# A dual-stream attention block on one core: where the text V gets its shift, where the text gate's rows are computed, and the order of three weight loads

## The chip, the core and the metric

The kernel runs on one core of a Trainium2 chip. The metric is the device time of one execution in microseconds (us). Five runs of the kernel before gave 118.70 to 119.60 us, median 119.28 us. One more execution was recorded by the hardware profiler; it took 118.92 us, of which the trace spans 116.8 us.

The engines are called as in the profile: PE is TensorE (matmuls), PEld its loading of weights, DVE is VectorE, ACT is ScalarE, POOL is GpSimd and SP is SyncE, which issues most of the DMAs. PSUM is the memory that matmuls write to, SBUF the one that everything else works in.

## What is computed

Two streams of tokens, image (2 x 256 tokens) and text (2 x 32 tokens), of width D = 1152, attend to each other. For each stream a conditioning vector c gives a shift, a scale and a gate; the normalised tokens are scaled and shifted, projected to Q, K and V, attended jointly, projected again, gated, and added to the input.

```python
mod_i = (_silu(c) @ wmod_img).reshape(B, 6, 1, D)
mod_t = (_silu(c) @ wmod_txt).reshape(B, 6, 1, D)
shi, sci, gai = (mod_i[:, 0].copy(), mod_i[:, 1].copy(), mod_i[:, 2].copy())
sht, sct, gat = (mod_t[:, 0].copy(), mod_t[:, 1].copy(), mod_t[:, 2].copy())
hi = _layernorm(x_img, axis=-1) * (1 + sci) + shi
ht = _layernorm(x_txt, axis=-1) * (1 + sct) + sht
qkvi = hi @ wqkv_img
qkvt = ht @ wqkv_txt
...
scores = jnp.einsum('bqd,bkd->bqk', q, k) * D ** (-0.5)
p = _softmax(scores, axis=-1)
a = jnp.einsum('bqk,bkd->bqd', p, v)
at, ai = (a[:, :Nt].copy(), a[:, Nt:].copy())
out_i = x_img + gai * (ai @ wo_img)
out_t = x_txt + gat * (at @ wo_txt)
```

All matrices are bfloat16. The weights that are read come to some 37 MB of the 39.4 MB that the core reads in all.

## The kernel before, in words

**Weights.** Fourteen blocks of 1152 x 1152 are read once each, into five slots of SBUF that are used again and again (`wtile(slot)`). All are issued on SP's queue, in the order of lines 103 to 122; an issue whose slot is still being read waits, and all later ones wait behind it. `load_w` (L89) issues a block whole or in column pieces, `load_rows` (L97) in three pieces of three row groups. The last five are `w_ga_i` (image gate, slot 0), `w_v_t` (text V, slot 1), `w_ga_t` (text gate, slot 2), `w_o_i` (image output, slot 3) and `w_o_t` (text output, slot 1 again).

**Order of work.** All matmuls go through `mm` (L61) and all transposes through `tr` (L64), which keep TensorE in program order. The other engines are put in order by the framework; where `pin` is written the program's order holds there too. The stages of TensorE are: image V (to 34 us), image Q and K in 18 groups of nine matmuls of 512 columns (`qk_img`), with text work hung between the groups (the `hooks`), text Q and K (`qk_txt`), scores, text V, attention, output.

**The text shift.** The row of the text shift is not made on TensorE: `vec_part` multiplies and adds the weights on VectorE, 18 operations on 128 x 1152 into `acc_sh` (L417, L419), in three parts that are hooks. `vec_split` cuts the sum into two bfloat16 halves (L426 on ACT, L427 on VectorE), which 16 small matmuls (`vec_rows`) bring into a row form. The text layernorm (`txt_ln`) and its transposes are two more hooks.

**The shift of V.** Image V is computed from the scaled input without the shift; its contribution `svc`, the shift times the V weights, is added to the attention's result when that leaves PSUM (L610, L612): each row of probabilities sums to one, so the shift passes through. Text V is computed from the shifted input, and so must have the image's `svc` taken away first. `shift_v_rows` keeps that row as `svr`, in PSUM's layout of four groups of columns. In `v_txt` the product of `hT_t` and `w_v_t` is followed by two matmuls per half with `sel`, a matrix of 0 and -1, that subtract `svr` inside PSUM (L489); four copies, alternating between VectorE (L184) and ACT (L186), bring the result to `v_t`, and L494 copies it to partitions 64 to 127.

**Tiled matmuls.** Where only 64 or 32 columns of TensorE are needed, two or four matmuls are given different column tiles (`tile_position`): text V and the text output two of 64 columns, the gates' rows and the shift rows four of 32 columns.

**The gates.** `mod_rows` (L496) makes a gate's row from `sT32` (the silu of c, padded to 32 columns) with 36 matmuls, copies it to SBUF and writes it to a DRAM scratch `gsc` (L505) from POOL's queue; DMAs on the same queue then spread it: `gb` for the image (L514), `gbf` for the text (L523). `xf` is the text input in the layout of the text output (L519).

**After the scores.** Softmax (`softmax_tile`, L542 to L551) leaves probabilities in four image tiles and `pbt` for the text. `p_transposes(b)` transposes nine blocks for one image b and copies them to `pT`, on VectorE for image 0 (L595), on ACT for image 1 (L597). Attention runs in three groups: six key matmuls on `v_i`, then six on `v_t`, then six more on `v_i`. The output follows: `out_img` for four tiles of 128 tokens, each three groups of nine matmuls of 384 columns, which VectorE multiplies with the gate (L650) and adds to the input (L651). The text output `out_txt` stands between the third and the fourth.

Of the kernel before, what the change touches and what calls it, by code (L numbers as in the profile page):

```python
# [14 lines left out]
def kernel(  # L15
# [14 lines left out]
    nc = tc.nc  # L30
    bf = mybir.dt.bfloat16
    f32 = mybir.dt.float32
    PSUM = bass.MemoryType.PSUM

    B, NI, D = x_img.shape
    NT = x_txt.shape[1]
    P = 128
    KT = D // P
# [3 lines left out]
    NTT = B * NT  # L42
    CH = 384
    NCH = D // CH
    VC = 288
# [5 lines left out]
    act = ctx.enter_context(tc.tile_pool(name="act", bufs=1))  # L51
    const = ctx.enter_context(tc.tile_pool(name="const", bufs=1))
    work = ctx.enter_context(tc.tile_pool(name="work", bufs=2))
    small = ctx.enter_context(tc.tile_pool(name="small", bufs=4))
    ps_mm = ctx.enter_context(tc.tile_pool(name="ps_mm", bufs=6, space=PSUM))
    ps_tr = ctx.enter_context(tc.tile_pool(name="ps_tr", bufs=2, space=PSUM))
# [3 lines left out]
    def mm(*a, **k):  # L60
        return pin(nc.tensor.matmul(*a, **k))  # L61
# [22 lines left out]
    def load_w(slot, src, c0, splits=(D,)):  # L84
        t = wtile(slot)
        sv = wview(src, c0)
        o = 0
        for n in splits:
            nc.sync.dma_start(t[:, :, o:o + n], sv[:, :, o:o + n])  # L89
            o += n  # L90
        return t

    def load_rows(slot, src, c0):
        t = wtile(slot)
        sv = wview(src, c0)
        for r0 in range(0, KT, 3):
            nc.sync.dma_start(t[:, r0:r0 + 3, :], sv[:, r0:r0 + 3, :])  # L97
        return t
# [13 lines left out]
    w_q_i = load_w(3, wqkv_img, 0)  # L112
    w_sh_t = load_rows(0, wmod_txt, 0)
    w_k_i = load_w(4, wqkv_img, D)
# [2 lines left out]
    w_k_t = load_w(3, wqkv_txt, D)  # L117
    w_ga_i = load_w(0, wmod_img, 2 * D)
    w_v_t = load_w(1, wqkv_txt, 2 * D)
    w_ga_t = load_w(2, wmod_txt, 2 * D)  # L120
    w_o_i = load_rows(3, wo_img, 0)
    w_o_t = load_rows(1, wo_txt, 0)

    nc.scalar.preload_act_table_set("natural_log_exp_and_others")
# [4 lines left out]
    NGG = 4  # L129
    LW = P // NGG  # L130
# [11 lines left out]
    sT32 = const.tile([P, KT, 32], bf)  # L142
# [39 lines left out]
    def evac(out_ap, in_ap):  # L182
        if evac_idx[0] % 2 == 0:
            nc.vector.tensor_copy(out_ap, in_ap)  # L184
        else:
            nc.scalar.copy(out_ap, in_ap)  # L186
        evac_idx[0] += 1
# [39 lines left out]
    def mod_cols_of(gps, name):  # L227
        t = const.tile([P, KT, LW], f32, name=name, tag={"shtc": "scc", "sctc": "shc"}.get(name, name))
        pin(nc.vector.transpose(t[:].rearrange("p c l -> p (c l)"), gps[:].rearrange("p c l -> p (c l)")))
        return t  # L230
# [141 lines left out]
    def qk_img(wq, blk, hooks):  # L372
        for j in range(KT):
            for hook in hooks.get(j, ()):
                hook()
            ps = ps_mm.tile([P, B * NI], f32, tag="mm")
            for kt in range(KT):
                mm(ps[:], lhsT=wq[:, kt, j * P:(j + 1) * P], rhs=hT_i[:, kt, :],
                   start=(kt == 0), stop=(kt == KT - 1))
            qk_evac(qkT[:, blk * KT + j, :, 0:NI], ps[:].rearrange("p (b n) -> p b n", b=B), blk)  # L380

    gsc = tc.dram_tile([2, B, D], bf, name="mod_scratch")
    sel = const.tile([P, NGG, NTT], bf)
    nc.gpsimd.tensor_scalar(sel[:].rearrange("p g (b t) -> p g b t", b=B),
                            ident[:].rearrange("p (g r) -> p g r", g=NGG)[:, :, 0:B].unsqueeze(3)
                            .to_broadcast([P, NGG, B, NT]), -1.0, None, op0=ALU.mult)
    v_t = act.tile([P, D], bf)
    svr = act.tile([P, KT, LW], bf)
    rows, cols = {}, {}

    def shift_v_rows():
        p_sv = mod_rows_of(w_v_i, shT32)
        nc.scalar.copy(svr[:], p_sv[:])
        cols["v"] = mod_cols_of(p_sv, "svc")

    xT_t = act.tile([P, KT, NTT], bf)
# [44 lines left out]
    def txt_shift_part(r0, r1):  # L441
        return lambda: vec_part(nc.vector, w_sh_t, acc_sh, r0, r1, range(B))
# [38 lines left out]
    def v_txt():  # L481
        for r in range(2):
            ps = ps_mm.tile([P, KT, LW], f32, tag="mm")
            for kt in range(KT):
                for g in range(2):
                    mm(ps[64 * g:64 * g + NTT], lhsT=hT_t[:, kt, :], rhs=group(w_v_t, kt, 2 * r + g),
                       start=(kt == 0), stop=False, tile_position=(0, 64 * g))
            for g in range(2):
                mm(ps[64 * g:64 * g + NTT], lhsT=sel[:, 2 * r + g, :], rhs=svr[:],  # L489
                   start=False, stop=True, tile_position=(0, 64 * g))  # L490
            for g in range(2):
                evac(v_t[0:NTT, :].rearrange("p (c g l) -> p g c l", g=NGG, l=LW)[:, 2 * r + g],
                     ps[64 * g:64 * g + NTT])
        nc.vector.tensor_copy(v_t[64:64 + NTT, :], v_t[0:NTT, :])  # L494

    def mod_rows(w_blk, si):  # L496
        gps = ps_mm.tile([P, VC], f32, tag="mm")
        for kt in range(KT):
            for g in range(NGG):
                mm(gps[32 * g:32 * g + 32, :], lhsT=sT32[:, kt, :], rhs=w_blk[:, kt, g * VC:(g + 1) * VC],  # L500
                   start=(kt == 0), stop=(kt == KT - 1), tile_position=(0, 32 * g))
        g_sb = work.tile([P, VC], bf, tag="garow")
        evac(g_sb[:], gps[:])
        for b in range(B):
            nc.gpsimd.dma_start(gsc[si, b, :].rearrange("(g j) -> g j", g=NGG), g_sb[b:P:32, :])  # L505

    gb = act.tile([P, B, D], bf, tag="Bt")
    gbf = act.tile([P, 2, VC], bf)
    xf = act.tile([P, 2, VC], bf)

    def img_gate():
        mod_rows(w_ga_i, 0)
        for b in range(B):
            nc.gpsimd.dma_start(gb[:, b, :], gsc[0, b, :].partition_broadcast(P))  # L514

    def txt_gate():
        mod_rows(w_ga_t, 1)
        for g in range(2):
            pin(nc.gpsimd.dma_start(xf[64 * g:64 * g + NTT, :, :],  # L519
                                    xt_flat.rearrange("t (r g j) -> g t r j", r=2, g=2)[g]))  # L520
            for b in range(B):
                r0 = 64 * g + 32 * b
                nc.gpsimd.dma_start(gbf[r0:r0 + NT, :, :],  # L523
                                    gsc[1, b, :].rearrange("(r g j) -> g r j", r=2, g=2)[g].partition_broadcast(NT))

    v_last()
    shift_v_rows()
    qk_img(w_q_i, 0, {1: (txt_ln,), 2: (txt_shift_part(0, 3),), 5: (txt_shift_part(3, 6),),
                      6: (txt_transposes,), 8: (txt_shift_part(6, KT),)})
    qk_img(w_k_i, 1, {1: (txt_shift_split,),  # L530
                      6: (txt_rows_scale, txt_rows_shift, txt_cols_shift, txt_modulate),
                      8: (lambda: qk_txt(0, w_q_t),)})
    qk_txt(1, w_k_t)
# [21 lines left out]
    def scores_img(b):  # L555
        for qi in range(TPB):
            q0 = qi * P
            sps = ps_mm.tile([P, NTOK], f32, tag="mm")
            for ft in range(KT):
                mm(sps[:], lhsT=qkT[:, ft, b, q0:q0 + P], rhs=qkT[:, KT + ft, b, :],  # L560
                   start=(ft == 0), stop=(ft == KT - 1))
            softmax_tile(sps, P, (b, qi), [(0, P, b)])
# [15 lines left out]
    def p_transposes(b):  # L578
        pT_ps = ps_tr.tile([P, 8 * P], bf, tag="tr")

        def one(kj, pb, qp, perm):
            o = kj * NTOK + qp
            tr(pT_ps[:, o:o + P], pb[:, kj * P:(kj + 1) * P], perm[:])

        for kj in range(3):
            if b:
                one(kj, pbs["t"], qpos[b][2], ident2)
            for qi in range(TPB):
                one(kj, pbs[(b, qi)], qpos[b][qi], ident)
            if not b:  # L590
                one(kj, pbs["t"], qpos[b][2], ident)
        pT_v = pT_ps[:, 0:3 * NTOK].rearrange("p (k n) -> p k n", k=3)
        pT = work.tile([P, 3, NTOK], bf, tag="pT")
        if b == 0:
            nc.vector.tensor_copy(pT[:], pT_v)  # L595
        else:
            nc.scalar.copy(pT[:], pT_v)  # L597
        pTs[b] = pT
# [29 lines left out]
    scores_img(0)  # L628
    scores_txt()
    img_gate()  # L630
    scores_img(1)
    v_txt()
    p_transposes(0)
    p_transposes(1)
    txt_gate()
    for d0 in range(0, KT, 3):
        attn_pair(*[[(b, dt) for dt in range(d0, d0 + 3)] for b in range(B)])

# [17 lines left out]

    def out_txt():
        of = work.tile([P, 2, VC], bf, tag="of", bufs=1)
        for r in range(2):
            ps = ps_mm.tile([P, VC], f32, tag="mm")  # L660
            for dt in range(KT):
                for g in range(2):
                    c0 = (2 * r + g) * VC
                    mm(ps[64 * g:64 * g + NTT, :], lhsT=aT[:, dt, NI:NI + NTT], rhs=w_o_t[:, dt, c0:c0 + VC],
                       start=(dt == 0), stop=(dt == KT - 1), tile_position=(0, 64 * g))
            tmp = work.tile([P, CH], bf, tag="tmp")
            nc.vector.tensor_mul(tmp[:, 0:VC], ps[:], gbf[:, r, :])
            nc.vector.tensor_add(of[:, r, :], tmp[:, 0:VC], xf[:, r, :])
        for g in range(2):
            eng = nc.sync if g == 0 else nc.scalar  # L670
            eng.dma_start(ot_flat.rearrange("t (r g j) -> g t r j", r=2, g=2)[g], of[64 * g:64 * g + NTT, :, :])
# [37 lines left out]
```

## Time and profile before

| what | value |
|---|---|
| five runs | 118.70, 118.78, 119.28, 119.31, 119.60 us |
| profiled execution | 118.92 us, span 116.8 us |
| TensorE clock granted | full throughout |
| image Q and K, text Q and K | 34.3 to 76.2 us |
| scores and image gate | 76.0 to 82.5 us |
| text V | 82.5 to 85.1 us |
| transposes of the probabilities | 85.1 to 86.2 us |
| text gate's rows | 86.2 to 87.4 us |
| attention | 87.4 to 93.1 us |
| image output, three tiles | 93.1 to 106.4 us |
| text output | 106.7 to 109.05 us |
| image output, last tile | 109.05 to 113.4 us |
| DMA read, written | 39.38 MB, 1.34 MB |

The stages are TensorE's, from the timeline. In a line of the timeline stand: start, length, engine, source line, operation, what is written and read, shapes, how many instructions; and in brackets how long the engine had been idle before it and what released it. Matmul lines can overlap by a few tenths, since their ends are modelled; the loads of weights (PEld) are the steadier mark of where TensorE is.

### The profile page before, as it was taken

How to read it: one execution, taken by the hardware profiler on the slowest of the kernel's cores; microseconds unless marked ns; L12 is line 12 of the kernel's file. 1: busy time of each engine (PE TensorE's matmuls, PEld its weight loads, DVE VectorE, ACT ScalarE, POOL GpSimd, SP SyncE). 2: the span in 40 equal slices, each digit the busy share in tenths (PEclk: the TensorE clock that was granted, in tenths of full speed). 3: DMA queues.
4: the chain of work that ended last, by engine and by line, in shares of the span. 5: the costliest groups of instructions: out<-in, count | busy, mean ns of one | idle time of the engine just before them, and what ended most of it. 6: DMA issues, size and time to landing. Idle time of an engine off the chain costs nothing.

```text
span 116.8 us, 2512 instructions
## 1 busy us (share of the span) xinstructions
PE 110.6 (95%) x1046; PEld 63.8 (55%) x1054; DVE 75.8 (65%) x161; ACT 41.8 (36%) x87; POOL 11.2 (10%) x34
## 2 busy tenths in 40 slices
PE   4997999999999999999999999999999999999990
PEld 2344644445674445444444557877875656666660
DVE  2588593072956799999999740027786846666671
ACT  5799700050852524432319233336454700000000
POOL 7420000000000000000000000002227026000000
PEclk9999999999999999999999999999999999999999
DMA  3999999999999999999999999999999999520223
GB/s 120 365 380 394 390 404 410 415 409 412 412 380 391 412 411 410 406 412 413 413 411 412 403 406 410 412 406 413 406 409 409 408 395 390 189 101 6 101 51 101
DMA packets 18613, 40.86 MB, mean 350 GB/s; under 512 B 1019, under 2 KB 1547, under 8 KB 18603
## 3 DMA queue, kind: packets, MB, share of 16 engines
q1 hardware_dynamic: 17728, 39.56, 87.3%
q0 software_dynamic: 480, 0.89, 2.2%
q10 hardware_dynamic: 395, 0.26, 0.7%
q8 instruction: 8, 0.13, 0.4%
q14 instruction: 2, 0.02, 0.0%
HBM read 39.38 MB, written 1.34 MB: 349 GB/s over the span
## 4 chain that ended last, share of the span: by engine, by line
PE 70%; DMA 21%; SPq 4%; DVE 1%; issue 1%; DVEq 0%
PE ps L61 50%; PE vps L61 15%; DMA t<-in_wo_img_dram 13%; DMA t<-in_wmod_img_dram 8%; PE gps L61 4%; SPq L97 3%; PE sc_ps L61 1%; SPq L104 1%; PE tp L64 1%; DVE tmp L650 1%; DVE o L651 0%; SPq L108 0%; PE tpt L64 0%; DVE hS_i L268 0%; DVE scc L261 0%
## 5 line engine op out<-in xcount | busy, mean ns | idle before, releaser
L61 PE MATMUL ps<-xT_i,t 128*128 128x512 bf16 x157 | 35.4, 379 | 0.3
L61 PEld LDWEIGHTS <-t 128*128 128x128 bf16 x324 | 20.5, 98 | 19.2 <-issue 0.5
L419 DVE SCALAR_TENSOR_TENSOR acc_sh<-t,sTf,acc_sh 128x1152 f32<-128x1152 bf16 x16 | 21.4, 1413 | 0.0
L61 PE MATMUL ps<-t,aT 128*128 128x384 bf16 (+3 forms) x153 | 20.3, 307 | 0.1
L61 PE MATMUL vps<-t,hS_i 128*128 128x512 bf16 (+1 forms) x106 | 17.8, 325 | 0.2
L61 PEld LDWEIGHTS <-aT 128*128 128x128 bf16 (+1 forms) x153 | 13.0, 101 | 7.4 <-issue 0.9
L61 PEld LDWEIGHTS <-hS_i 128*128 128x128 bf16 x108 | 9.0, 98 | 8.8 <-DVE hS_i L268 0.4
L650 DVE TENSOR_TENSOR tmp<-ps,gb 128x384 bf16<-128x384 f32 (+2 forms) x13 | 6.8, 526 | 6.6 <-PE ps L61 6.6
L368 ACT ACTIVATE qkT<-ps 128x512 bf16<-128x512 f32 (+2 forms) x11 | 6.2, 561 | 11.9 <-PE ps L61 11.9
L370 ACT CAST qkT<-ps 128x512 bf16<-128x512 f32 (+2 forms) x11 | 5.9, 553 | 11.0 <-PE ps L61 11.0
L505 POOL DMA_DIRECT2D mod_scratch<-g_sb x4 | 2.5, 636 | 74.6 <-ACT g_sb L186 74.5
L61 PE MATMUL wps<-warm 128*128 128x512 bf16 x24 | 7.3, 459 | 1.7 <-DVE unit L132 1.5
L184 DVE CAST v_i<-vps 128x512 bf16<-128x512 f32 x5 | 3.5, 692 | 7.5 <-PE vps L61 7.5
L542 DVE TENSOR_REDUCE nmx<-sps 128x1 f32<-128x288 f32 x4 | 1.7, 450 | 8.9 <-PE sps L61 8.9
L61 PEld LDWEIGHTS <-sT 128*32 128x32 bf16 x180 | 4.6, 96 | 2.6 <-issue 1.8
L186 ACT CAST v_i<-vps 128x512 bf16<-128x512 f32 x4 | 2.3, 580 | 9.9 <-PE vps L61 9.9
L61 PE MATMUL sps<-qkT 128*128 128x288 bf16 (+1 forms) x54 | 5.5, 287 | 0.0
L610 DVE TENSOR_SCALAR aT<-aps,svc 128x288 bf16<-128x288 f32 x9 | 4.3, 517 | 1.6 <-PE aps L61 1.6
L61 PE MATMUL gps<-t,sT 128*32 128x288 bf16 x144 | 5.2, 287 | 0.0
L61 PEld LDWEIGHTS <-warm 128*128 128x128 bf16 x25 | 2.5, 112 | 4.9 <-issue 1.9
L61 PE MATMUL aps<-pT,v_i 128*128 128x288 bf16 x36 | 5.1, 287 | 0.0
L61 PE MATMUL ps<-hT_t,t 128*128 128x64 bf16 x162 | 5.0, 193 | 0.0
(112 smaller groups left out, 107.6 us busy)
## 6 DMA issues: line engine op xcount, KB each, us to landing
t<-in_wqkv_txt_dram SPq DMA_DIRECT2D x3, 2592.0 KB, 18.1
t<-in_wmod_img_dram SPq DMA_DIRECT2D x2, 2592.0 KB, 12.5
t<-in_wqkv_img_dram SPq DMA_DIRECT2D x2, 2592.0 KB, 20.4
t<-in_wmod_txt_dram SPq DMA_DIRECT2D x2, 2592.0 KB, 16.7
t<-in_wmod_txt_dram SPq DMA_DIRECT2D x3, 864.0 KB, 14.9
t<-in_wo_img_dram SPq DMA_DIRECT2D x3, 864.0 KB, 13.7
t<-in_wo_txt_dram SPq DMA_DIRECT2D x3, 864.0 KB, 13.2
t<-in_wqkv_img_dram SPq DMA_DIRECT2D x3, 576.0 KB, 9.4
```

The lines of the kernel that those rows point to most:

```text
L61: return pin(nc.tensor.matmul(*a, **k))
L64: return pin(nc.tensor.transpose(*a, **k))
L97: nc.sync.dma_start(t[:, r0:r0 + 3, :], sv[:, r0:r0 + 3, :])
L184: nc.vector.tensor_copy(out_ap, in_ap)
L186: nc.scalar.copy(out_ap, in_ap)
L368: nc.scalar.mul(out_ap, in_ap, SCALE)
L370: nc.scalar.copy(out_ap, in_ap)
L419: pin(eng.scalar_tensor_tensor(acc[:, b, :], w[:, kt, :], sTf[:, kt, b:b + 1], acc[:, b, :], op0=ALU.mult, op1=ALU.add))
L505: nc.gpsimd.dma_start(gsc[si, b, :].rearrange("(g j) -> g j", g=NGG), g_sb[b:P:32, :])
L542: nc.vector.reduce_max(nmx[0:qn, :], sps[0:qn, :], axis=AX.X, negate=True)
L610: nc.vector.tensor_scalar(dst, tiles[(b, dt)][:], bias, None, op0=ALU.add)
L650: nc.vector.tensor_mul(tmp[:, 0:n], ps[:, 0:n], gb[:, b, c0:c0 + n])
```

## The change

Four things are changed.

- The load of `w_o_i` is issued ahead of that of `w_ga_t`.
- Text V: the two `sel` matmuls per half are gone. The row `svr` is written to a DRAM scratch early, in `shift_v_rows`, and spread over the partitions of the text tokens by four DMAs into `svb`. Four subtractions on VectorE take the product out of PSUM and subtract `svb` at once. `p_transposes(0)` now stands before `v_txt`.
- The text gate: its 36 matmuls move into `out_txt`. Its row is not sent through DRAM: matmuls with `sel` spread it over the partitions in PSUM (`gate_of`), and ACT copies it to `gbf`, with the sign turned. The text output's matmuls now are four of 32 columns in place of two of 64. The `xf` loads are issued by themselves (`txt_x`).
- The hooks between the Q and K groups: the first part of the text shift stands before the layernorm, and the transposes stand in the K row.

```diff
+    w_o_i = load_rows(3, wo_img, 0)
     w_ga_t = load_w(2, wmod_txt, 2 * D)
-    w_o_i = load_rows(3, wo_img, 0)
     w_o_t = load_rows(1, wo_txt, 0)
...
+    svd = tc.dram_tile([B, 2, 2, KT * LW], bf, name="sv_scratch")
+    svb = act.tile([P, 2, KT * LW], bf)
...
     def shift_v_rows():
         p_sv = mod_rows_of(w_v_i, shT32)
         nc.scalar.copy(svr[:], p_sv[:])
+        for b in range(B):
+            nc.gpsimd.dma_start(svd[b].rearrange("r g j -> (r g) j"), svr[b:P:32].rearrange("p c l -> p (c l)"))
+        for g in range(2):
+            for b in range(B):
+                r0 = 64 * g + NT * b
+                nc.gpsimd.dma_start(svb[r0:r0 + NT], svd[b, :, g, :].partition_broadcast(NT))
         cols["v"] = mod_cols_of(p_sv, "svc")
...
                 for g in range(2):
                     mm(ps[64 * g:64 * g + NTT], lhsT=hT_t[:, kt, :], rhs=group(w_v_t, kt, 2 * r + g),
-                       start=(kt == 0), stop=False, tile_position=(0, 64 * g))
+                       start=(kt == 0), stop=(kt == KT - 1), tile_position=(0, 64 * g))
             for g in range(2):
-                mm(ps[64 * g:64 * g + NTT], lhsT=sel[:, 2 * r + g, :], rhs=svr[:],
-                   start=False, stop=True, tile_position=(0, 64 * g))
-            for g in range(2):
-                evac(v_t[0:NTT, :].rearrange("p (c g l) -> p g c l", g=NGG, l=LW)[:, 2 * r + g],
-                     ps[64 * g:64 * g + NTT])
+                nc.vector.tensor_sub(v_t[0:NTT, :].rearrange("p (c g l) -> p g c l", g=NGG, l=LW)[:, 2 * r + g],
+                                     ps[64 * g:64 * g + NTT],
+                                     svb[64 * g:64 * g + NTT, r].rearrange("p (c l) -> p c l", l=LW))
         nc.vector.tensor_copy(v_t[64:64 + NTT, :], v_t[0:NTT, :])
...
-    qk_img(w_q_i, 0, {1: (txt_ln,), 2: (txt_shift_part(0, 3),), 5: (txt_shift_part(3, 6),),
-                      6: (txt_transposes,), 8: (txt_shift_part(6, KT),)})
-    qk_img(w_k_i, 1, {1: (txt_shift_split,),
+    qk_img(w_q_i, 0, {1: (txt_shift_part(0, 3),), 3: (txt_ln,), 4: (txt_shift_part(3, 6),),
+                      7: (txt_shift_part(6, KT),)})
+    qk_img(w_k_i, 1, {1: (txt_transposes, txt_shift_split,),
...
     img_gate()
+    txt_x()
     scores_img(1)
+    p_transposes(0)
     v_txt()
-    p_transposes(0)
     p_transposes(1)
-    txt_gate()
...
     def out_txt():
         of = work.tile([P, 2, VC], bf, tag="of", bufs=1)
-        for r in range(2):
+        gps = ps_tr.tile([P, VC], f32, tag="tr")
+        for kt in range(KT):
+            for g in range(NGG):
+                mm(gps[32 * g:32 * g + 32, :], lhsT=sT32[:, kt, :], rhs=w_ga_t[:, kt, g * VC:(g + 1) * VC],
+                   start=(kt == 0), stop=(kt == KT - 1), tile_position=(0, 32 * g))
+        g_sb = work.tile([P, VC], bf, tag="garow")
+        nc.scalar.copy(g_sb[:], gps[:])
+        quads = [(g, b, 64 * g + NT * b) for g in range(2) for b in range(B)]
+
+        def rows_of(r):
             ps = ps_mm.tile([P, VC], f32, tag="mm")
             for dt in range(KT):
-                for g in range(2):
+                for g, b, r0 in quads:
                     c0 = (2 * r + g) * VC
-                    mm(ps[64 * g:64 * g + NTT, :], lhsT=aT[:, dt, NI:NI + NTT], rhs=w_o_t[:, dt, c0:c0 + VC],
-                       start=(dt == 0), stop=(dt == KT - 1), tile_position=(0, 64 * g))
+                    mm(ps[r0:r0 + NT, :], lhsT=aT[:, dt, NI + NT * b:NI + NT * (b + 1)], rhs=w_o_t[:, dt, c0:c0 + VC],
+                       start=(dt == 0), stop=(dt == KT - 1), tile_position=(0, r0))
+            return ps
+
+        def gate_of(r):
+            gp = ps_tr.tile([P, VC], f32, tag="tr")
+            for g, b, r0 in quads:
+                mm(gp[r0:r0 + NT, :], lhsT=sel[:, 2 * r + g, NT * b:NT * (b + 1)], rhs=g_sb[:],
+                   start=True, stop=True, tile_position=(0, r0))
+            nc.scalar.mul(gbf[:, r, :], gp[:], -1.0)
+
+        def finish(r, ps):
             tmp = work.tile([P, CH], bf, tag="tmp")
             nc.vector.tensor_mul(tmp[:, 0:VC], ps[:], gbf[:, r, :])
             nc.vector.tensor_add(of[:, r, :], tmp[:, 0:VC], xf[:, r, :])
+
+        ps = rows_of(0)
+        gate_of(0)
+        gate_of(1)
+        finish(0, ps)
+        finish(1, rows_of(1))
```

## The prediction

> **What bounds the kernel now.** I read the page's first two parts, then the chain of waits in order of time, then the timeline from 76 us to the end, then the waits and landings of single transfers.
>
> ```profile
> PE 110.6 (95%) x1046; PEld 63.8 (55%) x1054; DVE 75.8 (65%) x161; ACT 41.8 (36%) x87; POOL 11.2 (10%) x34
> DMA  3999999999999999999999999999999999520223
> ```
>
> TensorE is busy for 95% of the span, and the DMA engines are full until about 99 us (34 slices of 2.92 us). So two things could set the end, and the chain has to say which.
>
> ```profile
> 76.68 2.71 SPq L97
> ...
> 79.45 14.96 DMA t<-in_wo_img_dram
> ...
> 94.45 18.70 PE ps L61 x138
> ```
>
> This is the end of the chain (start, length, what): before these lines it is TensorE's work, then come the image output weights, then TensorE's work nearly to the end. But the chain names only what ended last. How long TensorE stood, the timeline shows:
>
> ```profile
> 94.45 11.96 PEld L61 LDWEIGHTS <-aT 128*128 128x128 bf16 x74 [0.34 <-issue]
> ```
>
> The weight load behind these weights was idle for 0.34 us. The image output's matmuls run at 0.1625 us each (L650 evictions follow each other by 1.46 us, nine matmuls); without a wait the seventh of them, the first that needs the last third of the weights, would start at 93.19 + 6 x 0.1625 = 94.17 against 94.44. The DMA costs 0.27 us; all the rest is TensorE. So a change pays by what it takes off TensorE, or loses by what it makes TensorE wait for.
>
> The stretch that the change rebuilds, from the timeline:
>
> ```profile
> 82.43 0.50 DVE L551 TENSOR_SCALAR pbt<-e,rs 32x64 bf16<-32x64 f32 x2
> ...
> 82.96 0.82 DVE L542 TENSOR_REDUCE nmx<-sps 128x1 f32<-128x288 f32 x2
> ...
> 85.39 0.81 DVE L184 CAST v_t<-ps 64x288 bf16<-64x288 f32 x2
> ...
> 86.12 0.59 DVE L595 COPY pT<-pT_ps 128x864 bf16<-128x864 bf16 x1
> 86.18 0.98 PEld L61 LDWEIGHTS <-sT 128*32 128x32 bf16 x36
> ...
> 86.75 0.45 DVE L494 COPY v_t<-v_t 64x1152 bf16<-64x1152 bf16 x1
> ...
> 87.40 0.60 PEld L61 LDWEIGHTS <-v_i 128*128 128x128 bf16 x6 [0.24 <-DVE v_t L494]
> ...
> 88.24 0.11 PEld L61 LDWEIGHTS <-v_t 32*128 32x128 bf16 x6 [0.24 <-issue]
> ...
> 106.72 2.10 PEld L61 LDWEIGHTS <-aT 128*64 128x64 bf16 x36 [0.32 <-issue]
> ...
> 109.05 4.41 PEld L61 LDWEIGHTS <-aT 128*128 128x128 bf16 x36 [0.23 <-issue]
> ```
>
> The reader should see that the text gate's 36 matmuls (86.18 to 87.40) lie in the very time in which VectorE finishes pT and v_t (ready at 87.20). TensorE reaches the matmuls on v_t at 88.24 without having waited for them. The gate's rows cost time there, but they cover VectorE.
>
> **What the Trainium skill says.** "TensorE: Matmul & The Clock Gate", Measured speedup vs the span model: column tiles run beside each other at a few ns each. The trace agrees: 36 matmuls of 32 columns take 1.22 us (86.18 to 87.40), so a set of four takes about 0.1225 us and the switch the rest; the text output's 36 matmuls of 64 columns take 2.33 us, which is 18 pairs at 0.1225 us and 0.12 us. A pair and a set of four cost the same. "TensorEngine Tiling (Array Packing)", Key Properties: changing the tiling drains the array; the trace shows 0.23 to 0.24 us of idle weight load at each change. "VectorE: DVE Perf Modes", Two Vector instructions with no wait between them: an instruction whose start quadrant differs from the last one's is held until all before it are done. The trace agrees: the L551 pair (partitions 0 and 32) takes 0.50 us for two of 0.24, the v_t pair (same partitions) 0.81 for two of 0.44.
>
> **The change part by part**, against the profiled execution's own time, 118.92 us (span 116.8 and 2.1 around it).
>
> 1. Earlier stages, up to 76 us. VectorE now takes the first six operations of the text shift before the text layernorm. They need the first third of their weights, which lands 19.1 us after its issue at 17.55, at 36.65; before, the layernorm started at 36.33. The rest is the same work, and the same 0.60 us wait for ACT's rstd, so acc_sh and its halves end about 0.4 us later: 65.35 instead of 64.95 (the L427 pair, 62.29 + 2.66). TensorE's 16 matmuls on them start at 64.91 in four sets; the last needs the last half at 65.28. New wait: 0.13 us, taken; bounds 0 and 0.5. The transposes of the text move from one point of TensorE's row of 512-column groups to another, with the same switch: nothing. The four svb broadcasts and two small writes on POOL's queue are queued at about 35 us, ahead of mod_scratch, which goes out only at 81 us: nothing waits. They move about 0.15 MB, which the later gbf broadcasts no longer do.
>
> 2. The last w_v_t use to v_t. TensorE: scores end at about 82.5; p_transposes(0) now comes first and waits for pbt (82.93, L551), so it starts at about 83.0, 0.45 us idle that v_txt filled before. Nine transposes (18 took 1.11 us) make 83.55; v_txt with 18 sets (2.2 us) and a switch ends at about 85.95; the second nine end at about 86.6; six key matmuls (0.84 us) end near 87.4. Left out: two sel sets, 0.24 us, and the gate's 1.22 us.
> VectorE: in the changed order the pT copy (0.59) stands ahead of pb2 and pb3, so these end 0.6 us later than 85.48; the first v_t subtraction starts at 85.97 instead of 85.39. ACT took two of the four v_t evictions; now VectorE takes all four. A subtraction from PSUM with a bf16 operand has its nearest rows in L667 (0.46) and L573 (0.45, 64 partitions). They alternate between partitions 0 and 64, so by the skill's rule each is held: 4 x 0.465 = 1.86, to 87.83; bounds 1.56 (overlapped as the pair at 85.39) and 2.1. Then the copy of v_t, 0.45: 88.3. With the semaphore (0.05) TensorE starts on v_t at 88.38, and 88.51 with the 0.13 of part 1, against 88.24. So the 1.46 us of matmuls that left TensorE here become idle time, and 0.27 us more. Queued behind that weight load is the whole attention: nothing passes it. pT for the second image (ACT, 0.88 us) is ready at about 87.7 and hides behind it.
>
> 3. Image output weights. They are still issued at 76.26, when their slot is free, but the 2592 KB of w_ga_t no longer lie ahead of them: at 410 GB/s (the page's row of GB/s) they land about 6.5 us earlier. Gain: the 0.27 us, and no more, as TensorE is not there earlier. w_ga_t and w_o_t still end the stream at about 100 us (the last third is issued at 86.0 and lands 14.4 us later) and are first read at 106.4 and 107.5.
>
> 4. Text output. The rows of the gate come in here: 9 sets. The text rows go from pairs to fours: 18 sets as before. gate_of: two sets. Together 29 sets instead of 18: 11 x 0.1225 = 1.35 us more on TensorE, between two image outputs that bound the end. Bounds: 1.1 and 1.9. The ACT copy of the gate's rows (0.40 and 0.26 of latency) is hidden by rows_of(0), 1.10 us; should it come late, up to 0.5 us. ACT's two scalings lie beside rows_of(1); VectorE has 0.51 us idle in each 1.46 us here. The gbf broadcasts (on POOL until 98.4 us) go away; nothing waited for them: nothing. xf moves from behind mod_scratch to behind gb: nothing.
>
> Sum: 0.27 - 0.27 + 1.35 = +1.35 us, 120.27 against 118.92. The five runs of before have the mean 119.13 (median 119.28); with the same difference that is 120.5, which I take.
>
> **Rivals.**
> A, the forecast: the gate's matmuls move from a place where they covered VectorE to one where TensorE has no slack. +0.9 to +1.9 us; 120.5.
> B, worse: the gate is also exposed in the text output (0.45 us of ACT copy and latency not covered), and the halves of the shift come 0.5 us late. +1.35 + 0.45 + 0.4 and some of the upper bound of the subtractions, +0.25: 121.6. For it: the chain PE, ACT, PE, ACT, VectorE is new. Against: the 1.10 us of rows_of(0) lie in between.
> C, about the same: v_t is ready before TensorE wants it. Then TensorE reaches it at 87.4, 0.84 us earlier: -0.84 - 0.27 + 1.35 = +0.24, 119.4. For it: only four VectorE operations stand between. Against: they would have to end 0.9 us earlier than the sum of their rows, in the order that is fixed.
> D, the other side, faster: v_t is ready by 86.9, so no wait is left on it; the wait on pbt (0.45) is gone too; and each change of tiling costs the 0.23 us that the weight load shows, of which two fall away. -0.84 - 0.45 - 0.27 + 1.35 - 0.46 = -0.67: 118.5. It decides from v_t at about 87.2 on; against it speak the same rows, and that 1.22 us for 36 matmuls leaves only 0.12 us for a switch.
> That the weights do not come ahead is no case of its own: it would give back 0.27 us.
>
> **How the numbers follow.** A 0.64, B 0.12, C 0.16, D 0.08. A measurement of this kernel can tell about 0.5%, 0.6 us, from no change. Slower by more: A, B and a quarter of C, 0.80. Within: the rest of C and 0.01 of D, 0.13. Faster: 0.07. The range goes from 119.6 (half of C is left out) to 121.3 (half of B): about 0.2 left out with D. A's own range is 120.0 to 121.0.
>
> **What would show it.** A weight load of v_t that waits for VectorE v_t for 0.8 us or more; a first v_t matmul at 88.3 to 88.7; no wait at the image output's third weights; a text output of about 3.7 us instead of 2.33; the first halves' wait at 65 us of about 0.1. The prediction is wrong if the attention starts on v_t before 87.7, or if the text output adds less than 1 us.

## The result, and the profile after

The changed kernel takes 119.9 us in the median of 20 runs, the kernel before 119.0 us in 39 runs beside it. The ratio is 1.0066, 95% interval 1.0050 to 1.0081: 0.79 us slower (0.60 to 0.96). One of the 20 runs took 396.0 us; it counts as slow, and the ratio is that of the means of the fast runs. The forecast was slower, by 1.35 us.

The first two parts of the page of the changed kernel, engines with their busy time, and the share of the DMA engines in 40 slices:

```profile
PE 110.8 (94%) x1086; PEld 64.1 (54%) x1094; DVE 76.0 (64%) x162; ACT 42.5 (36%) x88; POOL 11.2 (9%) x34
DMA  4999999999999999999999999999999999422023
```

TensorE's busy time is the same to 0.2 us, and the span is 118.1 in place of 116.8. The work was moved, not lengthened; what came in is waiting. Pieces of the chain of waits say where (start, length, what):

```profile
77.80 0.47 DVE nmx L543
...
87.12 0.45 DVE v_t L497
87.57 0.01 issue
87.59 0.47 DVE v_t L497
...
88.08 0.47 DVE v_t L500
...
88.59 5.00 PE aps L61 x46
93.59 13.16 PE ps L61 x81
106.75 1.22 PE gps L61 x36
...
109.07 0.24 PE gp L61 x8
```

The image output weights are gone from the chain. It leaves TensorE at 77.78 us, at the first scores, and stays on VectorE and ACT, with the softmax and then VectorE's subtractions and copy of v_t, until TensorE takes it up again at 88.59. So whatever lengthens VectorE's row in these 11 us can move the attention. Further down the gate's rows (gps) and their spreading (gp) stand in it, between the image outputs. The weight loads and the subtractions, from the timeline:

```profile
86.20 1.85 DVE L497 TENSOR_TENSOR v_t<-ps,svb 64x288 bf16<-64x288 f32 x4
...
88.10 0.09 PEld L61 LDWEIGHTS <-v_t 32*128 32x128 bf16 x2 [0.93 <-DVE v_t L497]
...
88.59 0.10 PEld L61 LDWEIGHTS <-v_t 32*128 32x128 bf16 x4 [0.40 <-DVE v_t L500]
...
93.30 13.06 PEld L61 LDWEIGHTS <-aT 128*128 128x128 bf16 x81
...
106.68 0.98 PEld L61 LDWEIGHTS <-sT 128*32 128x32 bf16 x36 [0.32 <-issue]
...
110.34 4.41 PEld L61 LDWEIGHTS <-aT 128*128 128x128 bf16 x36 [0.24 <-issue]
```

Before v_t TensorE's weight loads stand 0.93 and then 0.40 us. Its matmuls stand 0.63 and 0.19 us there, by ends that are modelled. The 81 weight loads of three image output tiles run through without a gap. The text output lasts from 106.68 to 110.34.

The two profiles can be set against each other stage by stage. Two marks, the start of the text scale's row in both kernels and of the first image output in the kernel before:

```profile
63.80 0.98 PEld L61 LDWEIGHTS <-sT 128*32 128x32 bf16 x36 [0.42 <-issue]
...
93.07 1.03 PEld L61 LDWEIGHTS <-aT 128*128 128x128 bf16 x7
```

```profile
64.10 0.98 PEld L61 LDWEIGHTS <-sT 128*32 128x32 bf16 x36 [0.42 <-issue]
```

Up to the end of pbt (82.93 before, 83.36 after) the changed kernel is 0.43 us behind. It is late before any changed instruction, since its first weights ended TensorE's wait at 11.95 in place of 11.57, and at the text scale's row it is 0.30 behind. 0.12 more is lost between 66 and 76.5 us, where TensorE's work is the same and the granted clock 1.00; the lower clock of this execution (0.997 in the mean) falls into its last 8 us. In the fourteen profiles the time from the text scale's row to the first scores is 12.24 to 12.37 us in thirteen and 12.52 in one, which has the program of the kernel before up to there. So I put the 0.43 us down to the executions and not to the change. From there on:

| stage | before, us | after, us | difference |
|---|---|---|---|
| end of pbt to first image output | 82.93 to 93.07 | 83.36 to 93.30 | -0.20 |
| three image output tiles | 93.07 to 106.72 | 93.30 to 106.68 | -0.27 |
| text output | 106.72 to 109.05 | 106.68 to 110.34 | +1.33 |
| rest | | | 0.0 |

The sum is +0.86 us, inside the interval that the runs give. What remains to be shown is why 1.46 us of matmuls taken away ahead of the attention brought only 0.20.

### The profile page after: what moved, and what is told of

Its sections match the earlier page's. It is cut to its first block, busy times and chain, and to the rows that moved or that the text cites. A ratio compares the mean times of both kernels' runs of the same rounds, so it can differ in the third digit from the quotient of the medians.

```text
span 118.1 us, 2595 instructions
## 1 busy us (share of the span) xinstructions
PE 110.8 (94%) x1086; PEld 64.1 (54%) x1094; DVE 76.0 (64%) x162; ACT 42.5 (36%) x88; POOL 11.2 (9%) x34
## 4 chain that ended last, share of the span: by engine, by line
PE 76%; DMA 8%; DVE 7%; ACT 3%; issue 1%; SPq 1%; ACTq 0%; DVEq 0%
PE ps L61 50%; PE vps L61 15%; DMA t<-in_wmod_img_dram 8%; PE gps L61 5%; PE aps L61 4%; ACT e L546 2%; DVE nmx L543 1%; DVE v_t L497 1%; PE sps L61 1%; PE tp L64 1%; ACT xT_i L254 1%; SPq L104 1%; DVE rs L548 1%; DVE pb L550 1%; DVE tmp L651 1%
```

## The experiments

All are timed against the kernel before, with its runs on the same chip beside them. Microseconds are (ratio - 1) x 119.2. The changed kernel itself stands at +0.79. In traces, times are counted from the text scale's row on (63.80 before, 64.10 after), so that a late start of an execution does not count; 0.1 us can still be the execution's, as above. The diffs are excerpts.

### Text V alone, and the gate alone

The first kernel is the one before with `svb`, the four subtractions, and `p_transposes(0)` ahead of text V. The second is the changed kernel with the old text V put back, so that of the change it keeps the gate, the loads and the hooks:

```diff
 text V alone, against before
-    v_txt()
     p_transposes(0)
+    v_txt()
     p_transposes(1)
     txt_gate()
 gate alone, against the changed kernel
-                nc.vector.tensor_sub(v_t..., ps..., svb...)
+                mm(ps..., lhsT=sel[:, 2 * r + g, :], rhs=svr[:], start=False, stop=True, ...)
+                evac(v_t..., ps...)
-    p_transposes(0)
     v_txt()
+    p_transposes(0)
```

> The kernel before with the text V part alone (svb, four subtractions, first transposes ahead of text V); gate, loads and hooks as before. Theory (the gate's rows cover VectorE): v_t is ready near 88.1 us of the old time scale, TensorE comes to it at about 88.0, against 88.24; what is gained, 0.1 to 0.2 us, is given back at the image output weights, whose landing does not move. So -0.1 to +0.1 us against before. Rival (the subtractions on VectorE are themselves what costs): 0.3 us or more over before.

> The changed kernel with the old text V (sel matmuls, four copies shared by VectorE and ACT, transposes after it); gate rows in the text output, loads and hooks as changed. Theory (the cost is the pair: the cover taken away while VectorE's chain gets longer): v_t is ready at 87.2, TensorE comes to it at 87.0, a second matter of 0.2 us; -1.0 before the attention, -0.27 at the weights, +1.33 in the text output: 0.0 to +0.2 us against before. Rival (the gate in the text output is the cost by itself, whatever stands ahead): +0.8 to +1.3.

Measured: text V alone 1.0004 (0.9986 to 1.0022), +0.05 us; the gate alone 1.0054 (1.0033 to 1.0075), +0.64 us. The first is as the theory had it. The second lies between theory and rival (0.39 to 0.89 us), and the trace of the gate alone shows what the theory had left out (weight loads of the first key matmuls, and of those on v_t):

```profile
86.74 0.60 PEld L61 LDWEIGHTS <-v_i 128*128 128x128 bf16 x6 [0.68 <-DVE pT L590]
...
87.58 0.11 PEld L61 LDWEIGHTS <-v_t 32*128 32x128 bf16 x6 [0.24 <-ACT pT L592]
```

With the old text V it is not v_t but pT of the first image that comes late: the key matmuls wait for VectorE's copy of it, and stand 0.68 us. So the gate's rows had covered two waits, on pT and on v_t. Without them TensorE is on v_t only 0.63 us earlier (87.58 - 63.77 = 23.81 us behind the scale's row, against 24.44), not 1.22. The gate moved by itself makes up most of the cost, whichever chain VectorE has; that the two parts need each other, as the theory said, is not shown: 0.05 + 0.64 is 0.79 within the intervals. The 0.64 us include the new order of loads and the hooks, which this kernel keeps.

### What the attention waits for

Four changes to the changed kernel, each on v_t or on what TensorE does in the meantime. First, the copy of pT of the first image goes to ACT:

```diff
-        if b == 0:
-            nc.vector.tensor_copy(pT[:], pT_v)
-        else:
-            nc.scalar.copy(pT[:], pT_v)
+        nc.scalar.copy(pT[:], pT_v)
```

> The changed kernel with the copy of pT of the first image on ACT in place of VectorE. Theory (VectorE's row pT, pb, subtractions, v_t is what the attention waits for): v_t is ready 0.4 to 0.6 us earlier and the changed kernel gains as much: +0.2 to +0.4 us against before. Rival (pT of the second image on ACT is equally late, or the end is set elsewhere): no gain, +0.8 against before, or slower as ACT has both copies.

Measured: 1.0026 (1.0004 to 1.0047), +0.31 us; 0.48 less than the changed kernel. The timeline:

```profile
85.23 1.85 DVE L497 TENSOR_TENSOR v_t<-ps,svb 64x288 bf16<-64x288 f32 x4
```

```profile
87.63 0.10 PEld L61 LDWEIGHTS <-v_t 32*128 32x128 bf16 x4 [0.40 <-DVE v_t L500]
```

The second part of v_t is read 23.99 us behind the scale's row (63.64), against 24.49 in the changed kernel: 0.50 earlier, and the kernel gains about as much. Of the 0.50, some 0.12 lie ahead of the copy and are the executions'. VectorE's row is what TensorE waits for.

Second, the order of the subtractions. In the changed kernel they start at partitions 0, 64, 0, 64. A first try to order them otherwise,

```diff
-        for r in range(2):
-            ...
+        for g in range(2):
+            for r in range(2):
                 nc.vector.tensor_sub(...)
```

> The changed kernel with the four subtractions in the order of their partitions (two that start at partition 0, then two at 64) in place of alternating. Theory (an instruction that starts at other partitions than the last is held until that has ended): the four take about 1.65 us in place of 1.85, and the kernel gains 0.1 to 0.2 us: +0.6 to +0.7 against before. Rival (start to start is set by the operation alone): 1.85 us again, +0.8.

came to 1.0072 (1.0044 to 1.0100), +0.86 us. The framework had put the four back in the old order, so it is the changed kernel once more, and says nothing on the question. With `pin` around the subtraction, which holds the program's order:

> The changed kernel with the four subtractions held by the program in the order of their partitions (in the run on their order before, the framework had put them back as they were). Theory (start at other partitions than the last one's makes an instruction wait): of the three starts behind another subtraction two lose the hold, so the four take 1.65 to 1.75 us in place of 1.85, and v_t is ready 0.1 to 0.2 earlier. Rival (a subtraction of two tensors never overlaps with the next one): 1.85 us again and no gain, +0.8 against before.

Measured: 1.0039 (1.0019 to 1.0058), +0.46 us. The timeline and the chain of that run:

```profile
86.22 1.66 DVE L500 TENSOR_TENSOR v_t<-ps,svb 64x288 bf16<-64x288 f32 x4
```

```profile
86.30 0.72 DVE v_t L500 x2
87.02 0.01 issue
87.04 0.84 DVE v_t L500 x2
```

The four take 1.66 in place of 1.85 us. In the chain the two of one start partition are one piece, with a step of 0.02 us only between the pairs; in the changed kernel's chain, shown above, there is a step ahead of each. This is what "VectorE: DVE Perf Modes", Two Vector instructions with no wait between them, states; two holds fewer are 0.19 us here, some 0.1 us for each. The time gained, 0.33 us, is more than that, within the intervals.

Third, six more key matmuls into the time in which TensorE waits, in the first of the three attention groups:

```diff
         attn_keys(t0, True)
         t1 = {...}
+        if keys_first:
+            attn_keys(t1, True)
...
-            first, (b, dt) = key in t1, key
+            first, (b, dt) = key in t1 and not keys_first, key
```

> The changed kernel; in the first of the three attention groups the key matmuls of both images come before those on v_t, so six matmuls of 0.12 us fill the time in which TensorE waits for v_t. Theory (VectorE's v_t is what the attention waits for): 0.5 to 0.75 us less than the changed kernel, so +0.05 to +0.3 against before. Rival (something else, pT of the second image or PSUM, holds the attention at the same time): no gain, +0.8.

Measured: 1.0037 (1.0021 to 1.0054), +0.44 us: about half of what was expected. The weight loads of that run:

```profile
87.39 0.58 PEld L61 LDWEIGHTS <-v_i 128*128 128x128 bf16 x5 [0.42 <-issue]
...
88.21 0.19 PEld L61 LDWEIGHTS <-v_t 32*128 32x128 bf16 x6 [0.24 <-issue]
...
89.12 0.58 PEld L61 LDWEIGHTS <-v_i 128*128 128x128 bf16 x5 [0.46 <-issue]
```

The wait for v_t is gone: only the 0.24 us of the tiling change stand before it. But all six accumulators of the group now end at once, and the next group's keys stand 0.46 us. The pool that they come from has six buffers (`ps_mm`), and the six copies to aT have still to empty them, which fits; the profile names no releaser.

### The hooks, and the order of the loads

The changed kernel with the hooks as before, and the changed kernel with the two loads as before:

```diff
 hooks
-    qk_img(w_q_i, 0, {1: (txt_shift_part(0, 3),), 3: (txt_ln,), 4: (txt_shift_part(3, 6),), ...
+    qk_img(w_q_i, 0, {1: (txt_ln,), 2: (txt_shift_part(0, 3),), 5: (txt_shift_part(3, 6),), ...
 loads
-    w_o_i = load_rows(3, wo_img, 0)
     w_ga_t = load_w(2, wmod_txt, 2 * D)
+    w_o_i = load_rows(3, wo_img, 0)
```

> The changed kernel with the hooks of the Q and K groups as before. Theory of the forecast: the new hooks cost 0 to 0.13 us: +0.65 to +0.8 against before. Rival (the new hooks gain, since VectorE no longer waits for the text input): more than +0.8, up to 1.0 over the changed kernel's time of before.

> The changed kernel with the two loads in the old order again (text gate ahead of image output). Theory (order pays only the wait at the image output's last third): that wait is back, 0.27 us as before and 0.2 more because TensorE arrives 0.2 us earlier; so 0.3 to 0.5 us over the changed kernel, that is 1.1 to 1.3 us over the kernel before. Rival (the order of the loads is hidden): as the changed kernel, 0.8 us over before.

Measured: hooks back 1.0059 (1.0039 to 1.0079), +0.70 us: no difference. Loads back, in six runs, 1.0127 (1.0087 to 1.0168), +1.51 us (1.04 to 2.00), that is about 0.7 more than the changed kernel. The middle is more than expected, and the interval takes in what was expected (1.1 to 1.3). The wait is there, and longer than before the change:

```profile
93.27 1.03 PEld L61 LDWEIGHTS <-aT 128*128 128x128 bf16 x7
95.28 1.72 PEld L61 LDWEIGHTS <-aT 128*128 128x128 bf16 x11 [0.98 <-issue]
```

The seventh weight load's successor starts 31.07 us behind the scale's row (64.21), against 30.65 before (94.45 - 63.80): with the same order of loads the last third came 0.42 us later, and TensorE was there 0.21 us earlier. The svb broadcasts, 0.15 MB, have moved ahead of these weights; at the 410 GB/s of the profile that would be 0.36 us, an estimate. So the load order is worth about 0.7 us to the changed kernel by these six runs, of which the forecast counted 0.27. Why the weights came later is the next question.

### Is it the svb traffic?

The kernel before with the six DMAs added and their result unused, and the kernel before with the first two column groups of the first output tile interleaved (six row groups of both, then three of both), which lets TensorE want the last third 0.97 us later:

```diff
 traffic
+        for b in range(B):
+            nc.gpsimd.dma_start(svd[b]..., svr[b:P:32]...)
+        for g in range(2):
+            for b in range(B):
+                nc.gpsimd.dma_start(svb[r0:r0 + NT], svd[b, :, g, :].partition_broadcast(NT))
 interleave
+            for d0, d1 in ((0, 6), (6, KT)):
+                for k in range(2):
+                    rows(pss[k], chunks[k], k * CH, d0, d1)
```

> The kernel before with the six DMAs that write svr to DRAM and spread it into svb added, and svb not used: text V is as before. New theory (the 0.15 MB go ahead of all weights that are still to come): at 410 GB/s the text gate's weights and the image output's last third land 0.36 us later than before; the first were just in time and the second 0.27 us late, so +0.3 to +0.5 us against before. Rival, the forecast's own step (the traffic costs nothing): 0.0.

> The kernel before with only the first two column groups of the first image output tile interleaved. Theory: the 0.27 us of wait for the last third of the weights are hidden, -0.27 us. Rival (the wait is TensorE's own pace and not the DMA's): 0.0.

Measured: traffic 1.0019 (0.9998 to 1.0040), +0.23 us (-0.02 to 0.48); interleave 1.0013 (0.9988 to 1.0038), +0.15 us (-0.14 to 0.45). The first is inconclusive: a small cost is likelier than none. The second is a miss: a gain of 0.27 us is outside its interval. The profiles do not settle it, for in both TensorE stands at another place, ahead of the second image's scores (`qkT`):

```profile
80.67 2.08 PEld L61 LDWEIGHTS <-qkT 128*128 128x128 bf16 x18 [0.58 <-issue]
```

That is the traffic run; before, the same line has 0.24 us. TensorE comes to the weights 0.35 us later for it, and finds them there. In the interleave's profile, which is also the one with 12.52 us up to the first scores, it comes 0.63 us later. The same stall stands in the profiles of the interleave alone (0.59), of text V alone (0.59) and of the last kernel below (0.60), and not in the other ten profiles. These four are among the six kernels made from the kernel before; none of the eight made from the changed kernel shows it. In the chain it lies ahead of the image gate's last matmul; what it is stays open, and so does how often the wait at the weights is met at all. It is as long as the differences that these runs look for, so it may stand in their times too.

The landings of the last third, which the traces keep, do not settle it either. With the old order of loads they are, from the span's start, 94.41 us (before) and 93.42 (interleave) without the broadcasts, and 94.54 (traffic), 94.70 (text V), 95.10 and 94.72 (the two kernels below) and 95.24 (loads back) with them. All five are later than both, which fits a delay. But the two without are 1.0 us apart, and loads back is 0.7 later than traffic with the same broadcasts, so neither the size of the delay nor the broadcasts as its cause are shown.

### Two versions

Text V alone with the interleaved groups; and in it the text gate moved behind the first six key matmuls, where TensorE had stood in the changed kernel:

```diff
     p_transposes(0)
     v_txt()
     p_transposes(1)
-    txt_gate()
...
         attn_keys(t0, True)
+        if after_keys:
+            after_keys()          (txt_gate, in the first group)
```

> The kernel before with the text V part alone, and the first two column groups of the first image output tile interleaved: the first six row groups of both, then the last three of both, so that TensorE wants the last third of the weights 0.97 us later. Theory (text V's gain is given back at the weights): the 0.27 us of wait and the 0.1 to 0.2 of text V both stay: -0.3 to -0.5 us against before. Rival (TensorE gains nothing ahead of the attention, and the wait moves): 0.0.

> The run with text V alone and the two interleaved groups, and in it the text gate's 36 matmuls moved from ahead of the attention to behind its first six key matmuls (in a PSUM buffer of the transposes). Theory (there they stand in TensorE's wait for v_t, and their weights have landed): the 0.27 us that they waited for w_ga_t go; v_t starts near 24.4 us after the text scale's rows in place of 24.67. 0.2 to 0.3 us less than that run, so -0.5 us against before. Rival (the wait moves to the image output weights or to pT): -0.3 as that run.

Measured: 0.9976 (0.9956 to 0.9997), -0.29 us; and 0.9968 (0.9944 to 0.9992), -0.38 us. Both intervals end just below 1, so both are faster than the kernel before by little, if at all: the plain medians of the first one and of the kernel before, 119.11 and 119.15 us, are almost equal, and its profile shows no gain (117.2 - 64.21 = 53.0 us from the text scale's row to the end, and 53.0 before). The first has a wait that the second does not have, as the weight loads show, first of the one and then of the other:

```profile
86.82 0.98 PEld L61 LDWEIGHTS <-sT 128*32 128x32 bf16 x36 [0.27 <-DMA t<-in_wmod_txt_dram]
```

```profile
86.65 0.64 PEld L61 LDWEIGHTS <-v_i 128*128 128x128 bf16 x6
87.53 0.98 PEld L61 LDWEIGHTS <-sT 128*32 128x32 bf16 x36 [0.24 <-issue]
88.75 0.11 PEld L61 LDWEIGHTS <-v_t 32*128 32x128 bf16 x6 [0.24 <-DVE v_t L500]
```

In the second the gate's rows follow the keys at once, and when they are done v_t is there: the 0.93 and 0.40 us of the changed kernel are filled with the very matmuls that it had moved away. The 0.27 us that this should bring over the first version are not shown by the times (-0.38 against -0.29, with intervals of a quarter of a microsecond and more to either side).

## Why the prediction was right, and where its sizes were off

The direction, the place and the mechanism held: the gate's rows left a place where TensorE would otherwise wait, and came to one where it does not. Their move with the old text V cost 0.64 us, and what shortens or fills the wait in the changed kernel brings part of its loss back (0.48, 0.33 and 0.35 us).

The size was at the edge. +0.79 lies below the range that the forecast gave its own rival A (+0.9 to +1.9), and 119.9 below A's 120.0; that it falls into the whole range owes to the half of C that the range took in, and so something to luck. Of the signs named, the wait on v_t (0.93 us), the weights without a wait and the text output (3.66 us) came as said. The first v_t matmul did not: it starts at 88.10, and without the 0.43 us of the executions at 87.67, where 87.7 was to be the mark of a wrong prediction; the four matmuls behind the copy start at 88.16 on that scale. The terms:

- Text output (+1.35 forecast): +1.33. Eleven more sets of 0.1225 us. ACT's copy of the gate's rows was hidden by `rows_of(0)`, as said.
- Image output weights (-0.27): -0.27 between the two profiles, and the loads land 7.4 us after issue in place of 13.7 in the median. What the order is worth in the changed kernel was counted too low: about 0.7 us, with a wait of 0.98 us in the profile of the old order. Whether the svb broadcasts make that wait longer, where the forecast put them at nothing, is not shown.
- The hooks (+0.13): 0. The first third of the shift's weights was there as soon as the layernorm's input had been (36.63 - 36.33 is the 0.30 us by which the whole execution was behind), and the halves did not hold TensorE (the scale's and shift's rows take 1.71 us to the next group, 1.70 before).
- Start of the attention (+0.14 without the hooks): -0.20. This is the term that was mis-sized, and it has two parts. The four subtractions took 1.85 us, as forecast (1.86). But the insertion of the pT copy ahead of pb2 cost 0.38 us and not 0.6, as these lines of VectorE show, before and after:

```profile
84.14 0.16 DVE L547 RECIPROCAL rs<-rs 128x1 f32<-128x1 f32 x1 [0.35 <-ACT e L545]
84.34 0.35 DVE L549 TENSOR_SCALAR pb<-e,rs 128x256 bf16<-128x256 f32 x1
```

```profile
84.57 0.16 DVE L548 RECIPROCAL rs<-rs 128x1 f32<-128x1 f32 x1 [0.35 <-ACT e L546]
84.65 0.59 DVE L596 COPY pT<-pT_ps 128x864 bf16<-128x864 bf16 x1
85.15 0.34 DVE L550 TENSOR_SCALAR pb<-e,rs 128x256 bf16<-128x256 f32 x1
```

From the start of the reciprocal to the product with it were 0.20 us and are now 0.58. The copy starts while the reciprocal still runs, 0.08 us behind its start, and pb2 starts 0.50 us behind the copy's: 0.59 us of copy are overlapped at both ends. So v_t was whole 0.22 us earlier than forecast (88.16 in place of 88.38; the forecast's own rows add up to 88.33, and the trace has 0.03 us ahead of the copy of v_t and 0.06 behind it where 0.05 was counted). And two of the six matmuls on v_t do not need the copy to partitions 64 to 127: they run at 88.10, ahead of it, where the forecast took v_t as one thing. The weight loads of the next keys follow the last v_t part by 0.23 us (88.59 to 88.82) in place of 0.35 (88.24 to 88.59): 0.12 us more. The wait on pbt, forecast at 0.45 us, was about 0.3 us, spread over the transposes (their columns become ready in two steps), and hidden, since VectorE has v_t last in any case.

Two readings of the forecast were off, without weight in its sum. Not each change of tiling shows 0.23 to 0.24 us of idle weight load. Between the transposes and the gate's rows of the kernel before it is 0.10 us (86.08 to 86.18). And the last third of the text output's weights lands 15.5 us after its issue, at 101.5, not after 14.4; the text output reads its weights from 107.67 on, so nothing waits for it.

Of the rivals, C (v_t ready in time) and D fell with the 0.93 us wait; B fell too, as the gate in the text output was not late and TensorE's work behind the halves was not held. The step between 1.35 and 0.86 us is 0.34 us at the attention, 0.13 us at the hooks and 0.02 us in the text output.

## What to carry to other kernels

Before moving matmuls out of a busy stretch, ask what they cover: on an engine that is 95% busy, a block that stands on the chain can give back much less than its length, because another engine is just finishing something behind it. Here 1.46 us of matmuls gave back 0.20, and the gate's 1.22 us alone, with the old text V, gave back 0.63. The test is to lay the other engines' next results beside the stretch and strike the block out; and where a wait must remain, to look for work that needs none of what is waited for and put it there.

When a transfer is moved forward in a full DMA stream, do not put it at nothing: look which later landings are just in time. Here a delay by its bytes (an estimate, 0.36 us) was not shown, but one profile had the weights 0.42 us late. And before a difference of two landings is given a cause, see how far they lie apart between executions.

## What was not expected of the hardware

- The hold on VectorE was expected, its price was not known: four subtractions took 1.85 us with alternating start partitions and 1.66 us in pairs, about 0.1 us for each hold.
- A copy of 0.59 us put into VectorE's row delayed the rest by 0.38 us only, as it overlapped with the instruction before it and the one behind.
- A stall of 0.35 us ahead of the image gate's last matmul appears in four of fourteen profiles, with the same work around it as in the others. Its cause was not found.
- The last third of one and the same load landed up to 1.0 us apart in two executions whose programs are the same up to there (94.41 and 93.42 us).
